# First rows of w_sp split ahead of the token mixer's last tile, and the w_out and first z loads queued behind the transposes of those rows

## The chip, the cores and the metric

The kernel runs on one core of a Trainium2 chip. The metric is the device time of one execution, in microseconds (us); a kernel's time is the median of its runs. The engines are PE (matmul; PEld is its weight load), DVE (vector), ACT (activation), POOL and SP; nearly all DMAs of this kernel are issued by SP, one after the other, in the order of SP's instructions.

## The reference

Two kinds of layer alternate over x of shape 2048 x 640: a segmented attention `_A_ref` and a gated MLP `_B_ref`, each behind a layernorm and added to x, and this twice. The change touches the MLP alone:

```python
def _B_ref(x, w_in, w_sp, b_sp, w_out):
    z = _gelu(jnp.einsum("bsd,df->bsf", x, w_in))
    z1 = z[..., :Fh]                                   # Fh = 864
    z2 = _layernorm(z[..., Fh:], axis=-1)
    g = jnp.einsum("ts,bsf->btf", w_sp, z2) + b_sp[None, :, None]
    return jnp.einsum("bsf,fd->bsd", z1 * g, w_out)

x = x + _A_ref(_layernorm(x), ...)
x = x + _B_ref(_layernorm(x), B_w_in, B_w_sp, B_b_sp, B_w_out)
x = x + _A_ref(_layernorm(x), ...)
x = x + _B_ref(_layernorm(x), B_w_in, B_w_sp, B_b_sp, B_w_out)
```

`w_sp` is 2048 x 2048 and mixes the tokens, so all of z2 has to be there before the first row of g is done.

## The kernel before

Every operand of a matmul is split into a high and a low f16 part, and a product is three matmuls (high by high, high by low, low by high). Each of the two layer pairs runs three phases, so that every phase runs twice; "first call" and "second call" below are the two calls of a phase.

`phase1a` is the attention. `phase1b` goes over 16 tiles of 128 tokens. For each it normalizes, turns the tile by a DMA transpose (`th`), and multiplies with the two halves of `w_in`: `w_in_half(1)` fills PSUM tile `zp1`, from which `z2_half` makes z2 (gelu on ACT, L301; layernorm on DVE with a power on POOL; the high part `zh` on ACT, L303; the low part `zl` on DVE, L304). `w_in_half(0)` fills `zp0`, from which `z1_half` makes z1 (gelu on ACT, L308) and stores it (L309, `z1_d[t]`). zh and zl of all 16 tiles stay in SBUF. The tile worked on last is number 11 (`ts`), called "the last tile" here. The profile leaves out buffer numbers, so it writes z for z1 and z2, zp for zp0 and zp1, cz for cz1, cx for cx1 and x for x1.

`phase2` goes over 16 tiles of 128 rows of w_sp.

- `rows(t)` loads 128 rows (`wr`, 1 MB, one buffer, L355), takes the largest magnitude of each row on DVE (`am`, L357), makes a power of two from it (`ivw`, L362), and splits the rows in two halves of 1024 columns: high part on ACT (`wn`, L367), low part on DVE (`wn`, L368), and one DMA transpose for each half (L369) that turns it into `wt` (two buffers).
- `spatial(t)` loads z1 of the tile (`cz1`, 432 KB, L375), multiplies `wt` with zh and zl (96 matmuls into `gp`, L380; k runs over the 16 token tiles, and the second half of wt is needed from k = 8), adds the bias on ACT (`u`, L383), multiplies with z1, splits the result like the rows (`un`, L393 and L394), and turns it by a DMA transpose (`ut`, L396).
- `tail(t)` loads x (`cx1`, 320 KB, L404), multiplies `ut` with w_out (42 matmuls into `cyp`, L409), adds x and stores.

In `phase2`, rows(0) is recorded first, under a high priority; then w_out is loaded (`g.wu.load`): in the first call as seven pieces `wst` through two buffers, which ACT and DVE split (L72, L73) and SP stores away for the second call (L111, L113); in the second call as the four stored parts (L96, L98; 960 + 120 KB for each of `wuh` and `wul`, 2.2 MB in all). Then spatial(t), rows(t+1) and tail(t-1) follow for each t. In the first call the next attention's first work (`nxt.early`) is recorded from t = 8 on.

A scheduler sets the order on each engine, from priorities, dependences and a timing model; each engine and SP then work strictly in that order. In phase1a and phase1b the order on PE is as written. Tiles of phase2 lie partly in the space of phase1b's tiles, and the first instruction that writes such a place waits until phase1b's last reader is done. With each of SP's DMAs stand the semaphores it waits for; of these, two matter here: in the first call the second cz1 load (L375) waits for the last matmul of zp0 of the last tile, and in the second call the first w_out load (L96) waits for that matmul.

## Time and profile before

| | us |
|---|---|
| three runs | 2442.37, 2444.76, 2446.39 |
| median | 2444.76 |
| profiled execution, its time | 2440.32 |
| profiled execution, its span | 2438.6 |
| PE busy in the span | 2218.2 (91%) |
| phase2, first call: first matmul of `gp` | 863.79 |
| phase2, second call: first matmul of `gp` | 2045.13 |

The profiled execution took 2440.32 us, 1.7 us more than its span and 4.4 us less than the median of the runs. A row of the timeline gives the start in us from the span's start, the duration, engine, line, operation, output<-input, how many instructions are merged, and in brackets how long the engine sat idle before it and what ended that. SP rows carry the engine name SPq, and their duration is the time SP was held by the issue, not that of the transfer. A row of the windows gives, for a stretch, each engine's busy time and number of instructions, then the granted PE clock as a share of full speed, the mean busy share of the DMA engines, and what they moved in GB/s.

### The profile page before, as it was taken

The numbers are of one execution on the slowest core, as the hardware profiler recorded it, in microseconds if no ns is written. First come the engines' busy times: TensorE is split into PE (matmuls) and PEld (weight loads), VectorE is DVE, ScalarE is ACT, GpSimd is POOL, SyncE is SP. The second block draws the span as 40 slices with busy tenths as digits, with TensorE's granted clock in tenths as the row PEclk, the third lists the DMA queues.
The fourth block names the chain that finished last, engine by engine and source line by source line (L and its number), as shares of the span: only waits on it lengthen the run. The fifth ranks groups of instructions, "written<-read, shape, count | busy, mean of one in ns | idle before, by whom it ended". The sixth has DMA issues, their size and how long they took to land.

```text
span 2438.6 us, 50718 instructions
## 1 busy us (share of the span) xinstructions
PE 2218.2 (91%) x20682; PEld 1319.0 (54%) x20682; DVE 1434.3 (59%) x2766; ACT 1133.7 (46%) x1388; POOL 936.1 (38%) x728
## 2 busy tenths in 40 slices
PE   3698789999899989999997989999988997999998
PEld 2355455666555545555554556565654554555554
DVE  8668878777654555444326777877764452454441
ACT  3278777777632222212124988777762221121110
POOL 3168678888610100000002988887871010000000
PEclk9899999999999999999999999999998998999999
DMA  6824634344553488766445253443455345665762
GB/s 196 214 57 109 162 115 122 93 117 133 146 143 107 113 223 206 171 157 164 114 127 133 77 119 88 113 109 93 123 160 124 88 108 165 163 169 155 175 127 58
DMA packets 502505, 325.00 MB, mean 133 GB/s; under 512 B 408512, under 2 KB 443456, under 8 KB 497152
## 3 DMA queue, kind: packets, MB, share of 16 engines
q1 hardware_dynamic: 502272, 321.76, 51.4%
q8 instruction: 162, 2.65, 0.5%
q14 instruction: 71, 0.58, 0.1%
HBM read 148.25 MB, written 85.34 MB: 96 GB/s over the span
## 4 chain that ended last, share of the span: by engine, by line
PE 60%; DVE 11%; DMA 11%; ACT 7%; issue 5%; POOL 3%; SPq 3%; ACTq 0%; DVEq 0%; POOLq 0%
PE gp L380 16%; PE zp L295 14%; PE cyp L409 6%; PE pv L909 3%; PE yps L666 3%; PE kps L690 3%; DMA wr<-in_B_w_sp_dram 3%; PE vps L633 3%; PE mp L856 3%; PE qps L690 3%; ACT PH L882 2%; ACT P L865 2%; PE es L856 2%; POOL PL L883 2%; DVE mx L872 2%
## 5 line engine op out<-in xcount | busy, mean ns | idle before, releaser
L883 POOL TENSOR_TENSOR PL<-P,PH 128x1280 f16<-128x1280 f32 x248 | 649.8, 2621 | 155.2 <-ACT PH L882 145.6
L380 PE MATMUL gp<-zh,wt 128*128 128x432 f16 x2048 | 466.5, 348 | 24.0 <-DMA wt<-wn 24.0
L872 DVE TENSOR_REDUCE mx<-mp 128x2 f32<-128x1024 f32 (+3 forms) x512 | 409.4, 818 | 108.1 <-PE mp L828 106.2
L380 PEld LDWEIGHTS <-wt 128*128 128x128 f16 x3072 | 301.8, 98 | 286.5 <-DMA wt<-wn 25.7
L865 ACT ACTIVATE P<-es,sc 128x1024 f32<-128x1024 f32 (+1 forms) x384 | 370.3, 964 | 128.5 <-PE es L828 122.6
L882 ACT CAST PH<-P 128x1280 f16<-128x1280 f32 x256 | 320.5, 1253 | 19.0 <-PE pv L909 12.0
L295 PEld LDWEIGHTS <-th 128*128 128x128 f16 x1920 | 188.9, 99 | 177.8 <-issue 11.7
L380 PE MATMUL gp<-zl,wt 128*128 128x432 f16 x1024 | 272.8, 348 | 0.0
L395 POOL MEMSET un<- 128x64 f16 x32 | 4.8, 151 | 675.7 <-DMA ut<-un 588.9
L205 POOL TENSOR_TENSOR lnrs<-lnve,mhalf 128x1 f32<-128x1 f32 x96 | 58.6, 618 | 484.6 <-DVE lnve L204 459.6
L856 PEld LDWEIGHTS <-qk 60*128 60x128 f16 (+1 forms) x2048 | 93.0, 94 | 222.2 <-issue 155.1
L357 DVE TENSOR_REDUCE am<-wr 128x1 f32<-128x2048 f32 x32 | 73.2, 2286 | 214.7 <-DMA wr<-in_B_w_sp_dram 214.6
L383 ACT ACTIVATE u<-gp,bsp,un 128x864 f32<-128x864 f32 x32 | 34.2, 1068 | 355.5 <-PE gp L380 355.5
L409 PE MATMUL cyp<-wuh,ut 128*128 128x320 f16 (+1 forms) x896 | 166.8, 303 | 15.4 <-DMA ut<-un 15.4
L633 PE MATMUL vps<-wvh,xt 128*128 128x320 f16 x640 | 156.3, 310 | 22.5 <-DMA xt<-xnhl 13.8
L856 PE MATMUL es<-qk 64*128 64x512 f16 (+3 forms) x1024 | 135.2, 299 | 41.6 <-ACT P L865 26.9
L409 PEld LDWEIGHTS <-ut 128*128 128x128 f16 (+1 forms) x1344 | 132.6, 99 | 73.7 <-DMA ut<-un 17.4
L909 PE MATMUL pv<-vs,PL 128*128 128x41 f16 x2560 | 163.8, 181 | 7.3 <-POOL PL L883 4.5
L909 PE MATMUL pv<-vs,PH 128*128 128x41 f16 x2560 | 167.8, 182 | 1.2 <-DVE ab L925 1.2
L828 PEld LDWEIGHTS <-big 64*128 64x128 f16 x3072 | 141.7, 95 | 49.8 <-issue 3.1
L856 PE MATMUL mp<-qk 60*128 60x512 f16 (+3 forms) x1024 | 137.8, 306 | 31.1 <-DVE mx L872 28.6
L367 ACT ACTIVATE wn<-wr,ivw 128x1024 f16<-128x1024 f32 x64 | 71.9, 1144 | 194.6 <-DVE ivw L362 111.1
(182 smaller groups left out, 4138.5 us busy)
## 6 DMA issues: line engine op xcount, KB each, us to landing
wr<-in_B_w_sp_dram SPq DMA_DIRECT2D x32, 1024.0 KB
qk<-st SPq DMA_DIRECT2D x256, 120.0 KB
x<-x SPq DMA_DIRECT2D x56, 320.0 KB
z<-z SPq DMA_DIRECT2D x32, 432.0 KB
cz<-z SPq DMA_DIRECT2D x32, 432.0 KB
xt<-in_A_x_dram SPq DMA_DIRECT2D x32, 320.0 KB
st<-qhl SPq DMA_DIRECT2D x40, 256.0 KB
st<-khl SPq DMA_DIRECT2D x40, 256.0 KB
```

The lines of the kernel that those rows point to most:

```text
L295: nc.tensor.matmul(zp[:, n, :FHH], a[:, k, :], b[:, k, c:c + FHH], start=(k == 0 and j == 0), stop=(k == KD - 1 and j == 2))
L380: nc.tensor.matmul(gp[:, n, :FHH], wt[:, k // 8, a, k % 8, :], b[:, k, n * FHH:(n + 1) * FHH], start=(k == 0 and j == 0), stop=(k == NT - ...
L409: nc.tensor.matmul(yp[:, n, :320], a[:kn[k], k, :], b[:kn[k], k, n * 320:(n + 1) * 320], start=(k == 0 and j == 0), stop=(k == KO - 1 and ...
L633: nc.tensor.matmul(ps, a[:, k, c], b[:, k, n * 320:(n + 1) * 320], start=(i == 0), stop=(i == 14))
L690: nc.tensor.matmul(ps, a[:, k, c], b[:, k, :], start=(i == 0), stop=(i == 14))
L828: nc.tensor.matmul(out, g.big[r, 64 - 64 * s:192 - 64 * s], mk, start=False, stop=s == 1, skip_group_check=True)
L856: nc.tensor.matmul(out[:, h, o:o + w], a[r, ac], b[r, bc], start=o == 0, stop=False, skip_group_check=True)
L865: nc.scalar.activation(P[:, :, 512 * c:512 * c + ew], es[:, :, :ew], AF.Exp, scale=g.esc)
L872: nc.vector.tensor_reduce(self.mx[m][:, :, i], mp[:, :, o:o + w], AX.X, ALU.max)
L882: nc.scalar.copy(PH, P[:, h])
L883: (nc.gpsimd if h == 0 or n < self.N - self.TAIL else nc.vector).tensor_tensor(PL, P[:, h], PH, ALU.subtract)
L909: nc.tensor.matmul(pv[:, i, h, :], x[:, c:c + 128], v[:, j, h0 + h, :], start=(j == 0 and x is PH), stop=(j == i and x is PL), skip_group_ ...
```

## The change

The split of the first rows (both halves, ACT and DVE) is placed ahead of two instructions of the last tile of phase1b: the gelu of z2 on ACT and the layernorm's last step on DVE get a dependence on the split, which is one of order alone (no semaphore). The w_out load and the first spatial, and with them the first z load, are recorded so that their DMAs are issued behind the second transpose of the first rows.

```diff
 def layernorm(g, xt, out, d, nch, mult=1.0):
     mv, rs = layernorm_stats(g, xt, d, nch, mult)
-    g.nc.vector.tensor_scalar(out, xt, mv[:, 0:1], rs, ALU.subtract, ALU.mult)
+    return g.nc.vector.tensor_scalar(out, xt, mv[:, 0:1], rs, ALU.subtract, ALU.mult)
...
-            nc.scalar.activation(z2.rearrange("p (n c) -> p n c", n=2), zp[:, :, :FHH], AF.Gelu_apprx_tanh, scale=g.zi[1])
-            layernorm(g, z2, z2, FH, 2, ZS)
+            i = nc.scalar.activation(z2.rearrange("p (n c) -> p n c", n=2), zp[:, :, :FHH], AF.Gelu_apprx_tanh, scale=g.zi[1])
+            j = layernorm(g, z2, z2, FH, 2, ZS)
+            g.last = i.ins, j.ins
...
-                nc.scalar.activation(hl[:, 0], wr[:, c], AF.Identity, scale=ivw)
-                nc.vector.scalar_tensor_tensor(hl[:, 1], wr[:, c], ivw, hl[:, 0], ALU.mult, ALU.subtract)
-                nc.sync.dma_start(wt[:, i].rearrange("p l k c -> p (l k) c"), hl.rearrange("p l c -> p (l c)"), transpose=True)
-            return wt, un
+                done = (nc.scalar.activation(hl[:, 0], wr[:, c], AF.Identity, scale=ivw),
+                        nc.vector.scalar_tensor_tensor(hl[:, 1], wr[:, c], ivw, hl[:, 0], ALU.mult, ALU.subtract))
+                for ins, behind in zip(done, g.last):
+                    if t == 0:
+                        tc.add_manual_dep(behind, ins.ins.name, mybir.DependencyInfo(
+                            mybir.DependencyClass.NoSync, mybir.DependencyReason.DATA), reason="first rows lead")
+                last = nc.sync.dma_start(wt[:, i].rearrange("p l k c -> p (l k) c"), hl.rearrange("p l c -> p (l c)"), transpose=True).ins
+            return wt, un, last
...
         with tc.high_priority(offset=HP):
             wt = rows(0)
-        for _ in g.wu.load(sp, D):
-            pass
+        with tc.issue_after(wt[2]):
+            for _ in g.wu.load(sp, D):
+                pass
         pend = None
         for t in range(NT):
-            u = spatial(t, wt)
+            with tc.issue_after(wt[2]) if t == 0 else ExitStack():
+                u = spatial(t, wt)
```

No instruction is added or taken away; the scheduler places them in another order. From L302 on, a line of the changed kernel stands up to 7 lines later than before.

On ACT, at the end of phase1b in the first call, before (L303 is zh, L308 the gelu of z1, L301 that of z2, L367 the split of rows, L72 that of w_out):

```order
L308 ACTIVATE z_12835<-zp_12804,sc 128x864
L301 ACTIVATE z_12869<-zp_12838,sc 128x864
L303 CAST zh<-z_12869 128x864
L367 ACTIVATE wn<-wr,ivw 128x1024 x2
L308 ACTIVATE z_12914<-zp_12883,sc 128x864
L72 ACTIVATE wuh<-wst,iv 128x640 x6
L367 ACTIVATE wn<-wr,ivw 128x1024 x2
```

and with the change:

```order
L309 ACTIVATE z_12835<-zp_12804,sc 128x864
L368 ACTIVATE wn<-wr,ivw 128x1024 x2
L301 ACTIVATE z_12869<-zp_12838,sc 128x864
L309 ACTIVATE z_12914<-zp_12883,sc 128x864
L304 CAST zh<-z_12869 128x864
L72 ACTIVATE wuh<-wst,iv 128x640 x4
L368 ACTIVATE wn<-wr,ivw 128x1024 x2
```

The split of the first rows moves from behind the last tile's zh to ahead of its z2 gelu; zh of that tile now comes behind the z1 gelu; and four pieces of w_out instead of six stand ahead of the split of the second rows. DVE's order moves alike, with one difference: there, the third piece of w_out stands between the row maximum and `ivw` of the second rows.

On SP at the same place, before, each DMA with the semaphores it waits for (the number in a name is a buffer's; a DMAHW semaphore is that of an earlier DMA):

```order
L309 DMA z_0_10<-z_12835 128x864 [waits Activation_49]
L106 DMA wst<-in_B_w_out_dram 128x640 [waits DMAHW6_49,PE_49]
L106 DMA wst<-in_B_w_out_dram 128x640 [waits DMAHW7_49]
L375 DMA cz_13026<-z_0_0 128x864 [waits DMAHW2_49]
L375 DMA cz_13167<-z_0_1 128x864 [waits DMAHW4_49,DMAHW1_49,PE_49]
L404 DMA cx_13308<-x_0_0 128x640
L404 DMA cx_13497<-x_0_1 128x640 [waits DMAHW3_49]
L369 DMA_TRANSPOSE wt<-wn 128x16x128 [waits DVE_49]
L369 DMA_TRANSPOSE wt<-wn 128x16x128 [waits DMAHW5_49,DVE_49]
L309 DMA z_0_11<-z_12914 128x864 [waits DMAHW6_49,Activation_49]
```

and with the change:

```order
L310 DMA z_0_10<-z_12835 128x864 [waits Activation_49]
L409 DMA cx_13308<-x_0_0 128x640 [waits DMAHW6_49,DMAHW4_49,PE_49]
L409 DMA cx_13497<-x_0_1 128x640 [waits DMAHW7_49,DMAHW2_49]
L374 DMA_TRANSPOSE wt<-wn 128x16x128 [waits DVE_49]
L374 DMA_TRANSPOSE wt<-wn 128x16x128 [waits DMAHW1_49,DVE_49]
L310 DMA z_0_11<-z_12914 128x864 [waits Activation_49]
L106 DMA wst<-in_B_w_out_dram 128x640 [waits DMAHW3_49]
L106 DMA wst<-in_B_w_out_dram 128x640
L380 DMA cz_13026<-z_0_0 128x864 [waits DMAHW5_49]
L356 DMA wr<-in_B_w_sp_dram 128x2048 [waits DMAHW6_49]
L380 DMA cz_13167<-z_0_1 128x864 [waits DMAHW7_49]
```

The two x loads of the tails are in neither group that the change holds back, and now come first. The first of them takes over the wait on PE that the second cz load had: for the last matmul of zp0 of the last tile. The transposes of the first rows stand right behind it.

On SP in the second call, with the change:

```order
L310 DMA z_1_10<-z_28382 128x864 [waits Activation_49]
L409 DMA cx_28818<-x_1_0 128x640 [waits DMAHW6_49,DMAHW2_49,DMAHW0_49]
L409 DMA cx_29007<-x_1_1 128x640 [waits DMAHW3_49,PE_49]
L374 DMA_TRANSPOSE wt<-wn 128x16x128 [waits DVE_49]
L374 DMA_TRANSPOSE wt<-wn 128x16x128 [waits DMAHW5_49,DVE_49]
L310 DMA z_1_11<-z_28461 128x864 [waits Activation_49]
L96 DMA wuh<-w_uh 128x3840 [waits DMAHW7_49]
L98 DMA wuh<-w_uh 96x640
L96 DMA wul<-w_ul 128x3840 [waits DMAHW1_49]
L98 DMA wul<-w_ul 96x640 [waits DMAHW2_49]
L380 DMA cz_28536<-z_1_0 128x864 [waits DMAHW3_49]
L356 DMA wr<-in_B_w_sp_dram 128x2048 [waits DMAHW4_49]
```

Before, the four w_out loads and two cz loads stood ahead of the first transpose there, and the load of the second rows (L355) came right behind the store of z_1_11; now w_out and a cz load stand between that store and the second rows. Further on in the second call, the transpose of the first `ut` comes ahead of those of the third rows instead of behind them, and on PE the first `cyp` group comes right behind the second `gp` group instead of 11 matmuls into the third. In the first call, the transpose of the fourth `ut` comes ahead of a load of rows instead of behind it. From the eighth rows on, SP's order in phase2 is the same as before in both calls.

More of the change, by code (lines that the diff above doesn't have):

```diff
@@ L366, in rows @@
                 hl = ph.tile([128, 2, 1024], F16, tag="wn", name="wn")
-                nc.scalar.activation(hl[:, 0], wr[:, c], AF.Identity, scale=ivw)
-                nc.vector.scalar_tensor_tensor(hl[:, 1], wr[:, c], ivw, hl[:, 0], ALU.mult, ALU.subtract)
-                nc.sync.dma_start(wt[:, i].rearrange("p l k c -> p (l k) c"), hl.rearrange("p l c -> p (l c)"), transpose=True)
-            return wt, un
+                done = (nc.scalar.activation(hl[:, 0], wr[:, c], AF.Identity, scale=ivw),
[6 more added lines that the diff above has]
+            return wt, un, last
         def spatial(t, wt):
-            wt, un = wt
+            wt, un, _ = wt
             z1 = p2.tile([128, FH], F32, tag="z1", name="cz1")
```

## The prediction

> **What bounds the kernel now.** I read the page first, its busy shares and its chain of waits, and then its costliest groups.
>
> ```profile
> PE 2218.2 (91%) x20682; PEld 1319.0 (54%) x20682; DVE 1434.3 (59%) x2766; ACT 1133.7 (46%) x1388; POOL 936.1 (38%) x728
> ...
> PE 60%; DVE 11%; DMA 11%; ACT 7%; issue 5%; POOL 3%; SPq 3%; ACTq 0%; DVEq 0%; POOLq 0%
> ...
> L380 PE MATMUL gp<-zh,wt 128*128 128x432 f16 x2048 | 466.5, 348 | 24.0 <-DMA wt<-wn 24.0
> ...
> L409 PE MATMUL cyp<-wuh,ut 128*128 128x320 f16 (+1 forms) x896 | 166.8, 303 | 15.4 <-DMA ut<-un 15.4
> ```
>
> PE is busy 91% of the span, and in phase2 it waits for one thing only: DMA transposes, 24.0 us for `wt` and 15.4 us for `ut`, 39.4 us in all. What this change moves can win no more than that, and the slow starts that follow some of these waits. Next I read PE's timeline through both calls of phase2 and kept the rows with an idle time of over half a microsecond in brackets, and some without for the length of a group.
>
> ```profile
> 863.79 0.90 PE L380 MATMUL gp<-zh,wt 128*128 128x432 f16 x2 [7.37 <-DMA wt<-wn]
> 887.30 0.54 PE L380 MATMUL gp<-zh,wt 128*128 128x432 f16 x2 [3.78 <-DMA wt<-wn]
> 906.51 0.43 PE L409 MATMUL cyp<-wuh,ut 128*128 128x320 f16 x2
> 912.22 0.53 PE L380 MATMUL gp<-zh,wt 128*128 128x432 f16 x2
> 929.74 0.43 PE L409 MATMUL cyp<-wuh,ut 128*128 128x320 f16 x2
> 935.45 0.53 PE L380 MATMUL gp<-zh,wt 128*128 128x432 f16 x2
> 980.06 0.45 PE L409 MATMUL cyp<-wuh,ut 128*128 128x320 f16 x2 [3.70 <-DMA ut<-un]
> 1004.98 0.43 PE L409 MATMUL cyp<-wuh,ut 128*128 128x320 f16 x2
> ...
> 2045.13 0.90 PE L380 MATMUL gp<-zh,wt 128*128 128x432 f16 x2 [12.23 <-DMA wt<-wn]
> 2065.32 0.54 PE L380 MATMUL gp<-zh,wt 128*128 128x432 f16 x2 [0.61 <-DMA wt<-wn]
> 2087.39 0.45 PE L409 MATMUL cyp<-wuh,ut 128*128 128x320 f16 x2 [2.38 <-DMA ut<-un]
> 2133.66 0.45 PE L409 MATMUL cyp<-wuh,ut 128*128 128x320 f16 x2 [1.64 <-DMA ut<-un]
> 2159.88 0.31 PE L409 MATMUL cyp<-wuh,ut 128*128 128x320 f16 x1 [2.82 <-DMA ut<-un]
> ```
>
> An undisturbed `gp` group takes 929.74 - 912.22 = 17.52 us, a `cyp` group 935.45 - 929.74 = 5.71, a tile 23.23. The first group of the first call ran from 863.79 to 887.30 - 3.78 = 883.52, which is 19.73: 2.21 too long. The second took 906.51 - 887.30 = 19.21: 1.69 too long. From 980.06 to 1004.98 it is 24.92, again 1.69 over a tile. The first group of the second call took 2065.32 - 0.61 - 2045.13 = 19.58: 2.06 over. So a stall of 3.7 us or more costs about 2 us behind it as well; after 2.38 us there is nothing of the kind: 2133.66 - 2087.39 = 46.27 is two tiles less the 11 matmuls that already ran (46.46 - 2.01), plus the stall of 1.64, but for 0.2. It is the granted clock, 0.50 in the gap by the windows (row below).
>
> **The change part by part.** First call. The rows' split, in the timelines of ACT and DVE:
>
> ```profile
> 850.98 0.98 ACT L301 ACTIVATE z<-zp,sc 128x864 f32<-128x864 f32 x1 [4.50 <-PE zp L295]
> 855.91 2.18 ACT L367 ACTIVATE wn<-wr,ivw 128x1024 f16<-128x1024 f32 x2
> ...
> 851.99 1.12 DVE L202 BATCH_NORM_STATS2 lnst<-z 128x6 f32<-128x432 f32 x2 [5.85 <-ACT z L301]
> 857.08 2.48 DVE L368 SCALAR_TENSOR_TENSOR wn<-wr,ivw,wn 128x1024 f16<-128x1024 f32 x2
> ```
>
> Moved ahead of the last z2, the split's 2.18 us fit ACT's 4.50 idle, and its 2.48 us DVE's 5.85. I cost the move at nothing; without that cover it would delay the last tile's zh and zl, which PE reads only at k = 15, 16 us into the first group. The split is then done before 851 instead of at 857.08 + 2.48 = 859.6. The transposes, however, are SP's, here its timeline and the second rows' maximum on DVE:
>
> ```profile
> 851.46 5.31 SPq L375 DMA_DIRECT2D cz<-z  x2
> 856.81 0.91 SPq L404 DMA_DIRECT2D cx<-x  x2
> 858.40 5.63 SPq L369 DMA_TRANSPOSE wt<-wn  x2
> 866.43 0.52 SPq L355 DMA_DIRECT2D wr<-in_B_w_sp_dram  x1
> 880.94 4.25 SPq L369 DMA_TRANSPOSE wt<-wn  x1
> ...
> 873.98 2.29 DVE L357 TENSOR_REDUCE am<-wr 128x1 f32<-128x2048 f32 x1 [2.15 <-DMA wr<-in_B_w_sp_dram]
> ```
>
> The second cz load holds SP until 856.8, just after zp0's last matmul (863.79 - 7.37 = 856.42). The first cx load now has that wait, and both transposes are queued behind it. So they go out at about 856.4 + 2 x 0.45 = 857.3 instead of 858.40: all the early split buys is 1.1 us. From issue to use it was 863.79 - 858.40 = 5.39; the first group would start near 862.7 and end at 882.4. **Gain of the first group: 1.1** (0 to 1.5; the upper end if the two cz loads' traffic no longer slows it).
>
> The second group waits for the second rows. Their load now follows transposes to about 862.9, the z store, two w_out pieces and a cz load: issued near 865.4 rather than 866.43, but behind 0.44 + 0.66 + 0.44 MB instead of 0.44 + 0.66, so I let it land as now, 873.8. Then DVE's order bites: the third w_out piece stands ahead of `ivw`, and its load may go out only when the first piece is split (near 871.4), behind the rows and a cz load. At the rate of the windows (below) it lands near 875.5; ACT and DVE split it by 877.3, the rows' split starts at 877.5, the transpose goes out at 880 against 880.94. It took 887.30 - 880.94 = 6.36 to land, behind two stores of w_out parts (0.98 MB each); these now come later, so I take 5.14 (2065.32 - 2060.18, an undisturbed one below): start at 885.2, 2.1 earlier. The stall before it is 885.2 - 882.4 = 2.8, between 2.38 (clock kept) and 3.70 (clock lost), so I take half of the 1.69: 0.8 more. **Gain up to the second group's end: 2.9, of which 1.1 is the first group's** (-2 to 5: third w_out piece 5 us late, or none late).
>
> The fourth `cyp` stalled 3.70 and lost 1.69 of clock, 5.39, for a reason that its SP rows show:
>
> ```profile
> 971.06 0.38 SPq L355 DMA_DIRECT2D wr<-in_B_w_sp_dram  x1
> 971.54 2.68 SPq L396 DMA_TRANSPOSE ut<-un  x1
> ```
>
> Its transpose stood right behind a 1 MB load. It now stands ahead of it. Against that, the third rows' load goes out only behind the first `ut` transpose and the w_out stores, near 892.7, some 4 us later than now; following the chain on (load 7, maximum and split 5, pair of transposes 5), I find the third `wt` and the third and fourth `ut` each landing within about 1 us of when PE wants them. I take 3 us for these three. **Gain 2.4** (-3 to 5.4). First call: 2.9 + 2.4 = 5.3.
>
> Second call. SP's timeline shows what is ahead of the first transposes; DVE's row is the second rows' landing, and two windows show the DMA engines (the last three figures are clock, DMA share and GB/s):
>
> ```profile
> 2032.93 0.32 SPq L96 DMA_DIRECT2D wuh<-w_uh  x1
> ...
> 2035.69 9.45 SPq L369 DMA_TRANSPOSE wt<-wn  x2
> ...
> 2046.14 0.44 SPq L355 DMA_DIRECT2D wr<-in_B_w_sp_dram  x1
> ...
> 2060.18 5.09 SPq L369 DMA_TRANSPOSE wt<-wn  x2
> ...
> 2054.55 2.29 DVE L357 TENSOR_REDUCE am<-wr 128x1 f32<-128x2048 f32 x1 [18.50 <-DMA wr<-in_B_w_sp_dram]
> ...
> 2036.00:2038.00 2.00, 0.00 (x0) 0.00 (x0) 0.05 (x1) 0.00 (x0) 0.00 (x0) 0.50 1.05 403
> 2056.00:2058.00 2.00, 2.00 (x13) 1.07 (x12) 1.50 (x6) 0.32 (x1) 0.00 (x0) 1.00 0.00 0
> ```
>
> w_out (2.2 MB) and two cz loads, 3.1 MB, go out from 2032.93 and keep the transposes waiting for 9.45 us. With the change only one cx load is ahead: issue at 2033.4, landing 5.14 later at 2038.6 instead of 2045.13. The first group starts 6.5 us earlier. But the 3.1 MB are not gone: the z store, w_out and a cz load now stand ahead of the second rows' load. The pair lands by about 2042 (an estimate: 5.14 for the first half, some 3 more for the second), then 0.44 + 2.2 + 0.44 + 1.05 = 4.1 MB at 400 GB/s is 10.3 us, and with the rest of the path a landing near 2053.9, against 2054.55. The DMA engines were idle at 2056, so this is when they are done with the same work in another order. The second group then starts at 2054 + 10.77 (2065.32 - 2054.55) = 2064.7, only 0.6 earlier, while the first now ends at 2038.6 + 19.6 = 2058.2. The 12-us gap is cut in two of 5.7 and 6.5, and the second one loses clock that the 0.61 did not: -2.0. **Second group's end: 1.4 later** (4.8 later if the bytes move at 300 GB/s, to 0.6 earlier).
>
> A rule of the Trainium skill bears on these slow starts ("TensorE: Matmul & The Clock Gate", Part 1): PE falls to half clock after an idle window of about 3.4 us and needs about as long a busy one to rise. By it a slow start costs at most 1.7 us (an estimate, half of 3.4), where this trace has 1.69 to 2.21, and the 2.8-us stall of the first call would cost none, as 2.38 did here; the sum below would be 1.1 us better, 2433.7.
>
> The first `cyp` of the second call waited 2.38 for `ut`, and two later ones 1.64 and 2.82. SP's rows:
>
> ```profile
> 2083.36 1.54 SPq L396 DMA_TRANSPOSE ut<-un  x1
> 2085.00 1.03 SPq L355 DMA_DIRECT2D wr<-in_B_w_sp_dram  x1
> ...
> 2123.14 0.49 SPq L355 DMA_DIRECT2D wr<-in_B_w_sp_dram  x1
> ...
> 2124.28 6.84 SPq L396 DMA_TRANSPOSE ut<-un  x1
> ```
>
> The first `ut` went out at 2083.36, behind the third rows' pair. It now stands ahead of that pair, near 2066 (an estimate: some 8 us of ACT and DVE behind the first group's end), while PE asks for it at 2084: **gain 2.4** (0 to 2.4). The fourth rows' load, at 2085.00 behind that `ut`, then no longer waits for it and goes out near 2082; with the steps as long as they are, the fifth tile's chain comes 4 to 5 us ahead of before, PE's work 1 us. The third `ut` held SP for 6.84 us behind the load of 2123.14. Its stall of 1.64 and the next one's 2.82 would go but for some 0.8: **gain 3.7** (0 to 4.5). Second call: -1.4 + 2.4 + 3.7 = 4.7.
>
> **Sum.** 5.3 + 4.7 = 10.0 us. The profiled execution would take 2440.32 - 10.0 = 2430.3; the runs' median is 4.4 above it, so 2444.76 - 10.0 = 2434.8, predicted as 2435. Later phases only shift: the attention that follows starts from phase2's last tiles, and no stall of phase2 lies between 980 and its end in the first call. POOL's order changes only among its memsets of `un`.
>
> **The rivals.** *The wait only moves.* The first groups start earlier, the second ones as before, and the `ut` stalls stay, because they belong to a DMA queue that has the same bytes to move. For it: 856.42 as SP's release, and DMA idle at 2056 whatever the order. Against it: three of those stalls have a changed order. Price: 2.9 in the first call, -1.4 + 2.4 in the second, minus about 1 of new stalls: gain 3, 2441.8.
>
> *The second rows become the bound.* w_out stands ahead of them in both calls. In the first the third piece lands as late after its issue as the rows did (873.98 - 866.43 = 7.55, so at 879 instead of 875.5), which puts the transpose at 883.5 and the group at 889, 1.7 later than now; 0.4 of clock and 1 of new stalls come on top. In the second the 4.1 MB move at 300 GB/s, 4.8 lost, 2.4 won back at `ut`. Stalls at 980, 2133 and 2159 as before. Sum 3.1 + 2.4 = 5.5 slower, 2450. It decides once the second `wt` lands after about 888 and 2066. For it: DVE's and SP's new order, and the bytes that now stand ahead of the load. Against: the 403 GB/s that the row shows.
>
> *More.* All waits for `ut` go and the second group of the first call comes 5 earlier: 18 us, 2427.
>
> **How the numbers follow.** Forecast 0.55, the wait only moves 0.24, second rows bound 0.14, more 0.07. A change of this kernel under 0.2%, 4.9 us, can't be told from none. Within the forecast about 0.06 falls short of it, and of the first rival 0.04 passes it: faster 0.60, same 0.26, slower 0.14. Range: 2427, all terms at their upper ends, to 2447, between the two rivals; the forecast's own is 2430 to 2440.
>
> **What would show it.** In the profile of the changed kernel: the first-rows split on ACT right behind the z1 gelu near 846, and the transpose all the same at 857; first groups near 862.7 and, by the gap before them, 5.7 us behind phase1b's last matmul in the second call; half clock after that in the second group there; its `wt` landing 26 us after the first; no idle time at the fourth `cyp` of the first call. Wrong it would be if the transposes left before zp0's last matmul, if the second rows landed more than 3 us off, or if `ut` stalls of more than 3 us in a call remain.

## The result and the profile after

| | us |
|---|---|
| the change, median of 14 runs | 2445.00 |
| before, median of 14 runs beside it | 2444.53 |
| ratio, with its 95% interval | 0.9999 (0.9988 to 1.0011) |
| profiled execution of the change, its time and its span | 2445.33, 2443.6 |

The change makes no difference that can be measured. A second set of runs (e10 below) gave 0.9988 (0.9974 to 1.0002). The forecast was 10 us less than before. The median lies within the range on record, 2427 to 2447, but the gain that was forecast did not come: as the table further down shows, the second call gained what was expected, the first lost nearly as much, and the two cancel.

The page of the changed kernel, the lines that stand against the first ones of the prediction:

```profile
PE 2224.8 (91%) x20682; PEld 1323.1 (54%) x20682; DVE 1437.5 (59%) x2766; ACT 1134.6 (46%) x1388; POOL 936.9 (38%) x728
...
L385 PE MATMUL gp<-zh,wt 128*128 128x432 f16 x2048 | 468.0, 349 | 22.5 <-DMA wt<-wn 22.5
...
L414 PE MATMUL cyp<-wuh,ut 128*128 128x320 f16 (+1 forms) x896 | 168.1, 305 | 12.6 <-DMA ut<-un 12.6
```

PE's idle time at `wt` and `ut` fell from 39.4 to 35.1 us, so 4.3 us of waiting are gone. But PE was busy 6.6 us longer (2224.8 against 2218.2) with the same 20682 matmuls. Half of that, 3.3 us, falls in the two stretches of phase2 that the table below compares (156.9 to 158.9 us and 130.5 to 131.9); the other half falls ahead of phase2 and between its calls, in work that the change does not touch. Where the waits and the slow matmuls of phase2 are shows in PE's timeline through its two calls. Here and below, only the rows with a wait or the start of a group are shown:

```profile
868.78 0.90 PE L385 MATMUL gp<-zh,wt 128*128 128x432 f16 x2 [6.46 <-DMA wt<-wn]
890.64 0.54 PE L385 MATMUL gp<-zh,wt 128*128 128x432 f16 x2 [2.09 <-DMA wt<-wn]
908.17 0.43 PE L414 MATMUL cyp<-wuh,ut 128*128 128x320 f16 x2
916.30 0.54 PE L385 MATMUL gp<-zh,wt 128*128 128x432 f16 x2 [2.26 <-DMA wt<-wn]
935.51 0.43 PE L414 MATMUL cyp<-wuh,ut 128*128 128x320 f16 x2
985.02 0.45 PE L414 MATMUL cyp<-wuh,ut 128*128 128x320 f16 x2 [2.89 <-DMA ut<-un]
992.41 0.53 PE L385 MATMUL gp<-zh,wt 128*128 128x432 f16 x2
1013.16 0.71 PE L414 MATMUL cyp<-wuh,ut 128*128 128x320 f16 x2 [3.06 <-DMA ut<-un]
1020.45 0.53 PE L385 MATMUL gp<-zh,wt 128*128 128x432 f16 x2
1037.97 0.43 PE L414 MATMUL cyp<-wuh,ut 128*128 128x320 f16 x2
...
2047.91 0.90 PE L385 MATMUL gp<-zh,wt 128*128 128x432 f16 x2 [5.29 <-DMA wt<-wn]
2073.32 0.90 PE L385 MATMUL gp<-zh,wt 128*128 128x432 f16 x2 [6.40 <-DMA wt<-wn]
2093.11 0.43 PE L414 MATMUL cyp<-wuh,ut 128*128 128x320 f16 x2
2164.76 0.45 PE L414 MATMUL cyp<-wuh,ut 128*128 128x320 f16 x2 [1.80 <-DMA ut<-un]
```

The start of the first `gp` group less its idle time is the end of phase1b's last matmul: 868.78 - 6.46 = 862.32, and 2042.62 in the second call. Before it was 856.42 and 2032.90. Nothing that the change does lies ahead of 862.32 on PE; across the twelve profiles of this study that end lies anywhere from 854.75 to 862.32, and both of these have the early split (e4 and the change). So two profiles are compared by stretches that begin at one event. Counted from phase1b's end:

| start of | before | change | gained so far |
|---|---|---|---|
| first call: first `gp` group | 7.37 | 6.46 | 0.9 |
| second `gp` group | 30.88 | 28.32 | 2.6 |
| first `cyp` group | 50.09 | 45.85 | 4.2 |
| second `cyp` group | 73.32 | 73.19 | 0.1 |
| sixth `cyp` group | 171.78 | 175.65 | -3.9 |
| second call: first `gp` group | 12.23 | 5.29 | 6.9 |
| second `gp` group | 32.42 | 30.70 | 1.7 |
| fifth `cyp` group | 150.22 | 145.38 | 4.8 |

Behind the sixth `cyp` of the first call and the fifth of the second, the two profiles run in step. The second call gained 4.8 us, as forecast (4.7). The first call gained 4.2 up to its first `cyp` and then lost 8.1. In the sum 1 us is left, less than the runs can tell. A second profile of the change (e10) gives 174.8 and 145.4 for the last rows of the two calls, so these numbers repeat within about 1 us.

### The profile page after: what moved, and what is told of

It is laid out like the page before. It is cut to its first block, busy times and chain, and to the rows that moved or that the text cites. A ratio compares the mean times of both kernels' runs of the same rounds, so it can differ in the third digit from the quotient of the medians.

```text
span 2443.6 us, 50712 instructions
## 1 busy us (share of the span) xinstructions
PE 2224.8 (91%) x20682; PEld 1323.1 (54%) x20682; DVE 1437.5 (59%) x2766; ACT 1134.6 (46%) x1388; POOL 936.9 (38%) x728
## 4 chain that ended last, share of the span: by engine, by line
PE 62%; DVE 11%; DMA 10%; ACT 7%; issue 5%; POOL 3%; SPq 2%; ACTq 0%; DVEq 0%; POOLq 0%
PE gp L385 16%; PE zp L295 14%; PE cyp L414 6%; PE pv L916 3%; PE yps L673 3%; PE kps L697 3%; PE vps L640 3%; PE mp L863 3%; PE qps L697 3%; DMA wr<-in_B_w_sp_dram 2%; ACT PH L889 2%; PE es L863 2%; ACT P L872 2%; DVE mx L879 2%; DMA ut<-un 2%
```

## The experiments

Two numbers are given for each kernel: the starts of the sixth `cyp` group in the first call and of the fifth in the second, from phase1b's end. The ratios are to runs of the kernel before that were taken beside each set; their medians were 2444.53 us for the change, 2444.55 for e1 to e4, 2440.59 for e5 to e8 and 2442.78 for e9 and e10, so medians of different sets can't be compared directly.

| | first call | second call | median, us | ratio to before (95%) |
|---|---|---|---|---|
| before | 171.8 | 150.2 | | |
| the change | 175.7 | 145.4 | 2445.00 | 0.9999 (0.9988 to 1.0011) |
| e1, the split alone | 174.6 | 152.3 | 2446.08 (one run) | |
| e2, the hold-back alone | 177.5 | 148.5 | 2443.06 (one run) | |
| e3, second call only | 172.4 | 146.1 | 2440.12 | 0.9983 (0.9970 to 0.9996) |
| e4, third rows early | 175.4 | 147.0 | 2442.13 | 0.9992 (0.9977 to 1.0007) |
| e5, `ut` ahead of the rows' load | 166.7 | 144.3 | 2431.47 | 0.9961 (0.9946 to 0.9977) |
| e6, the same without the change | 166.9 | 144.0 | 2434.62 | 0.9965 (0.9951 to 0.9979) |
| e7, x loads held back too | 162.0 | 138.6 | 2423.29 | 0.9928 (0.9911 to 0.9944) |
| e8, all of it | 157.5 | 132.2 | 2408.55 | 0.9866 (0.9850 to 0.9882) |
| e9, e7 without the early split | 169.7 | 145.6 | 2434.52 | 0.9967 (0.9954 to 0.9981) |
| e10, the change again | 174.8 | 145.4 | 2439.78 | 0.9988 (0.9974 to 1.0002) |

### Which part does what: e1, e2, e3

e1 takes the hold-back out:

```diff
-        with tc.issue_after(wt[2]):
+        with ExitStack():
             for _ in g.wu.load(sp, D):
                 pass
...
-            with tc.issue_after(wt[2]) if t == 0 else ExitStack():
+            with ExitStack():
                 u = spatial(t, wt)
```

> Only the split of the first rows is moved ahead of the last tile; w_out and the z loads are not held back, so SP's order is that of before. Measured are, in the profile, the times from the last matmul of phase1b to the sixth cyp group of phase2's first call (before 171.8 us, change 175.7) and to the fifth cyp group of the second call (before 150.2, change 145.4). Theory (SP's order sets everything, the split is under cover): 171.8 and 150.2, each within 0.5, because the first transposes still stand behind w_out and the z loads. Rival 1 (the early split itself delays the last tile's z2 and with it zh and zl, which costs the first call what it lost): the first call 174 or more, with a stall of PE inside the first gp group at k = 15. Rival 2 (what was seen is one execution's chance): both numbers off by several us, in any direction.

Measured: 174.6 and 152.3. The theory's numbers were missed by 2.8 and 2.1, and rival 1 has the right number in the first call, but not by its mechanism: there is no stall inside the first group. PE's timeline of e1 shows what happened:

```profile
862.74 0.90 PE L385 MATMUL gp<-zh,wt 128*128 128x432 f16 x2 [7.44 <-DMA wt<-wn]
885.78 0.54 PE L385 MATMUL gp<-zh,wt 128*128 128x432 f16 x2 [3.36 <-DMA wt<-wn]
903.31 0.43 PE L414 MATMUL cyp<-wuh,ut 128*128 128x320 f16 x2
952.21 0.72 PE L414 MATMUL cyp<-wuh,ut 128*128 128x320 f16 x2 [2.28 <-DMA ut<-un]
959.55 0.53 PE L385 MATMUL gp<-zh,wt 128*128 128x432 f16 x2
```

and POOL's timeline of the kernel before dates the landing of the same `ut` there:

```profile
951.59 0.15 POOL L395 MEMSET un<- 128x64 f16 x1 [26.71 <-DMA ut<-un]
```

The first group starts as late as before (7.44 against 7.37): with the z loads ahead of the transposes, the early split buys nothing there. The second group's stall of 3.36 cost no clock (903.31 - 885.78 = 17.53, an undisturbed group), so the first `cyp` came 2.1 earlier than before. The third `cyp` then stalled for 2.28 and lost another 1.63 of clock (959.55 - 952.21 = 7.34 against 5.71). The end of PE's wait dates the landing of its transpose, 952.21. Where PE does not wait, POOL does: its memset of `un` can start only when the transpose that reads `un` is done, so a memset whose wait ended with that transpose dates the landing. Before, that was 951.59. Counted from phase1b's end, this `ut` landed at 95.2 before and at 96.9 in e1, and PE asked for it at 96.6 before and at 94.6 in e1. So it was late all along and covered by 1.4 us. Of the stall of 2.28, 0.5 was uncovered by the gain ahead of it; the other 1.7 is a later landing, because the transpose went out 1.8 later (88.4 against 86.6). Why it did is not shown. In the second call, 1.69 of the 2.1 is clock: PE waited 2.41 us at its first `cyp` and lost 1.69 behind it, where before it waited 2.38 and lost nothing.

e2 takes the early split out and keeps the hold-back:

```diff
                 for ins, behind in zip(done, g.last):
-                    if t == 0:
+                    if False:
```

> Only the hold-back: SP's order is that of the change, the split of the first rows stands where it stood before, behind the last tile's zh. Theory: the first call loses as the change did, 175.7 plus up to 2 (the split ends some 2 us later than SP is free for it); the second call 145.4 plus up to 3, for the same reason. So the hold-back explains the loss of the first call and nearly all of the gain of the second. Rival 1 (the early split makes the loss): the first call 172 or less. Rival 2 (the early split makes the gain of the second call): the second call near 150.

Measured: 177.5 and 148.5, at the upper end of what the theory allowed. The hold-back alone makes the loss of the first call, but only 1.7 of the 4.8 us that the second gains. With the early split on top, the change is 1.9 and 3.1 us better than e2 in the two calls.

e3 gives the first call the order of before:

```diff
+        second = g.wu.made
...
-        with tc.issue_after(wt[2]):
+        with tc.issue_after(wt[2]) if second else ExitStack():
...
-            with tc.issue_after(wt[2]) if t == 0 else ExitStack():
+            with tc.issue_after(wt[2]) if second and t == 0 else ExitStack():
...
-                    if t == 0:
+                    if t == 0 and g.wu.made:
```

> The change in the second call alone; the first call has the order of before on every engine. Theory (the two calls have opposite signs): first call 171.8 within 0.5, second call 145.4 within 0.5, and the median 4 to 5 us below the kernel before, a ratio of 0.998. Rival 1 (the second call's gain is given back behind the fifth cyp group, or in the rest of the program): ratio 1.000. Rival 2 (chance): the second call's number near 150.

Measured: 172.4 and 146.1, ratio 0.9983. Both numbers are 0.6 to 0.7 over the theory's, a little outside its half microsecond, and the ratio is as forecast. With the change in the second call alone, the kernel gains; that the first call loses rests on the stretches of the profiles (the change, e2 and e10), as the intervals of e3 and of the change overlap.

### What the first call loses: e4

SP's timeline in the first call of the change: the second and third rows' loads, and then three `ut` transposes with the load of rows that stands next to each.

```profile
862.35 0.79 SPq L409 DMA_DIRECT2D cx<-x  x2
863.20 5.54 SPq L374 DMA_TRANSPOSE wt<-wn  x2
...
871.81 0.43 SPq L356 DMA_DIRECT2D wr<-in_B_w_sp_dram  x1
...
885.72 3.14 SPq L374 DMA_TRANSPOSE wt<-wn  x1
...
900.45 1.00 SPq L356 DMA_DIRECT2D wr<-in_B_w_sp_dram  x1
...
952.62 1.57 SPq L401 DMA_TRANSPOSE ut<-un  x1
...
972.37 0.46 SPq L356 DMA_DIRECT2D wr<-in_B_w_sp_dram  x1
...
974.71 6.25 SPq L401 DMA_TRANSPOSE ut<-un  x1
...
1004.54 0.33 SPq L356 DMA_DIRECT2D wr<-in_B_w_sp_dram  x1
1005.60 1.31 SPq L401 DMA_TRANSPOSE ut<-un  x1
```

The landings of these three, by POOL's timeline:

```profile
956.71 0.15 POOL L400 MEMSET un<- 128x64 f16 x1 [2.08 <-DMA ut<-un]
985.11 0.15 POOL L400 MEMSET un<- 128x64 f16 x1 [28.25 <-DMA ut<-un]
1013.16 0.15 POOL L400 MEMSET un<- 128x64 f16 x1 [1.28 <-DMA ut<-un]
```

Two explanations offer themselves. One: the third rows' load left at 900.45, 38.1 us behind phase1b's end, where before it was 888.81 - 856.42 = 32.4, and all that follows is late. The other: a transpose lands late whenever a 1 MB load stands just ahead of it. The third `ut`, with the last such load 19.8 us ahead, took 956.71 - 952.62 = 4.1 us to land; the fourth, 2.3 us behind a load, took 10.4; the fifth, 1.1 us behind one, 7.6. e4 tells them apart. It puts the third rows' load ahead of the four stores of w_out (`g.wu.stores`) and of the first `ut` (`g.ut0`), and says nothing of the later loads and `ut`s:

```diff
-            nc.sync.dma_start(wr, w_sp[t * 128:(t + 1) * 128, :])
+            i = nc.sync.dma_start(wr, w_sp[t * 128:(t + 1) * 128, :]).ins
+            if t == 2 and g.wu.stores:
+                for behind in g.wu.stores + [g.ut0]:
+                    tc.add_manual_dep(behind, i.name, mybir.DependencyInfo(
+                        mybir.DependencyClass.NoSync, mybir.DependencyReason.DATA), reason="third rows lead")
+                g.wu.stores = []
```

> The change, and in the first call the load of the third rows stands ahead of the four stores of w_out and of the first ut transpose instead of behind them; the rest of SP's order to the tenth DMA behind is the same. Theory (the third rows' load, 5.7 us late, makes the stalls at the third gp group, 2.26, and at the fourth and fifth cyp, 2.89 and 3.06, and the slow clock behind them): the load goes out some 30 us behind phase1b's end instead of 38, these three stalls go but for 1 to 2 us in all, and the sixth cyp group starts at 168 to 170 instead of 175.7; the median 8 to 11 us below the kernel before (ratio 0.9955 to 0.997). Rival 1 (the stores of w_out and the ut transposes are what the queue is short of, and the wait only moves to the first ut): a new stall at the first or second cyp group and 174 to 176. Rival 2 (the stalls at the fourth and fifth cyp come from their own loads, not from the chain of the third): the stall of 2.26 goes, the others stay, 173.

Measured: 175.4, nothing gained. The load went out 30.0 us behind phase1b's end, as wanted, and the third `wt` no longer stalled. But these are SP's rows further on,

```profile
941.49 0.39 SPq L357 DMA_DIRECT2D wr<-in_B_w_sp_dram  x1
...
942.54 7.11 SPq L407 DMA_TRANSPOSE ut<-un  x1
```

PE's,

```profile
952.43 0.72 PE L422 MATMUL cyp<-wuh,ut 128*128 128x320 f16 x2 [5.41 <-DMA ut<-un]
982.04 0.45 PE L422 MATMUL cyp<-wuh,ut 128*128 128x320 f16 x2 [3.26 <-DMA ut<-un]
```

and POOL's:

```profile
952.52 0.15 POOL L406 MEMSET un<- 128x64 f16 x1 [26.65 <-DMA ut<-un]
```

Now the third `ut` stands 1.1 us behind a load, takes 952.52 - 942.54 = 10.0 us to land, and PE waits for it 5.41 us. The scheduler's order explains it: in e4 the loads of rows and the `ut` transposes stand on SP in the order of the kernel before, with the sixth rows' load just ahead of the third `ut`, the eighth just ahead of the fourth, and the fifth `ut` ahead of the ninth rows' load. So the third `ut` collides, the fourth still does (0.5 us behind a load, a stall of 3.26), and the fifth no longer does and has no stall. The theory of the late third rows falls but for the one stall at the third `wt`. Rival 2, that each stall belongs to the load next to it, is right about the cause; its number (173) took the loads to stay where they were, and missed that one collision went and a new one came.

### The collisions: e5 and e6

e5 keeps the change and queues the load of rows t+3 behind the transpose of `ut` t:

```diff
+        uts = []
+
+        def behind_ut(i, t):
+            if t >= 3:
+                tc.add_manual_dep(i, uts[t - 3].name, mybir.DependencyInfo(
+                    mybir.DependencyClass.NoSync, mybir.DependencyReason.DATA), reason="ut leads")
...
-            nc.sync.dma_start(wr, w_sp[t * 128:(t + 1) * 128, :])
+            behind_ut(nc.sync.dma_start(wr, w_sp[t * 128:(t + 1) * 128, :]).ins, t)
...
-            nc.sync.dma_start(ut.rearrange("p l k c -> p (l k) c"), hl.rearrange("p l c -> p (l c)"), transpose=True)
+            uts.append(nc.sync.dma_start(ut.rearrange("p l k c -> p (l k) c"), hl.rearrange("p l c -> p (l c)"), transpose=True).ins)
```

> The change, and in both calls the load of rows t+3 is issued behind the transpose of ut t. Theory (a ut transpose that is issued within 3 us behind a 1 MB load of rows lands 7.6 to 10.4 us after its issue, one with no load ahead of it 4.1; these collisions, not the third rows' load, cost the first call its gain): the stalls at the fourth and fifth cyp of the first call (2.89 and 3.06, with some 4 of slow clock) and the 1.80 in the second go, the third wt's 2.26 stays. Sixth cyp group of the first call 166 to 168 us behind phase1b's end (before 171.8, change 175.7), fifth of the second call 143.6 (before 150.2, change 145.4); ratio to before 0.995 to 0.997. Rival 1 (the rows' chain is the bound, and a later load makes wt late in the place of ut): new stalls at gp groups in the first eight tiles, 174 or more. Rival 2 (what is gained in the first tiles is lost behind them): the numbers as by the theory, but ratio 0.998 or more.

Measured: 166.7 and 144.3, ratio 0.9961, as the theory had it. The stalls of 3.06 and 1.80 are gone and that of 2.89 is down to 1.98, with no clock lost behind it. What is left of it is the same thing with smaller transfers: this `ut` landed 7.6 us behind its issue (973.27 to 980.85), right behind a store of x, a z load and two x loads, 1.4 MB in four pieces. Of the 9.0 us that the first call gained on the change, 1.8 are luck: the third `wt` stalled much as in the change (2.18), but with no slow clock behind it, for which the edit gives no reason.

e6 does the same edit to the kernel before.

> The kernel before, without the change, and with the load of rows t+3 issued behind the transpose of ut t. By the theory of the collisions, the stalls of 3.70 in the first call and of 1.64 and 2.82 in the second go: sixth cyp group 166.4 us behind phase1b's end (before 171.8), fifth of the second call 145.8 (before 150.2), ratio 0.996. Rival 1 (the rows' chain is the bound): new stalls at gp groups, 171 or more. Rival 2 (the collision is chance, and another transpose takes its place): some ut still lands over 7 us behind its issue.

Measured: 166.9 and 144.0, ratio 0.9965. PE's rows at the fourth `cyp` of the first call and at the first, third and fourth of the second, where before it waited 3.70, 2.38, 1.64 and 2.82:

```profile
977.39 0.44 PE L416 MATMUL cyp<-wuh,ut 128*128 128x320 f16 x2
...
2084.11 0.45 PE L416 MATMUL cyp<-wuh,ut 128*128 128x320 f16 x2 [0.60 <-DMA ut<-un]
2128.57 0.43 PE L416 MATMUL cyp<-wuh,ut 128*128 128x320 f16 x2
2151.80 0.43 PE L416 MATMUL cyp<-wuh,ut 128*128 128x320 f16 x2
```

In both calls no `ut` that can be dated lands over 6.7 us behind its issue, so rival 2 did not come. The order of the rows' loads and the `ut` transposes, with nothing else touched in the source, wins 0.35%, about 8.5 us, where the whole change was forecast to win 10. The collisions were there before the change; in the first call the change moved the tiles so that two of them met PE in the place of one.

### What holds the first transposes back: e7, e9

e7 is the change with the x loads of the first three tails queued behind the first transposes too:

```diff
             if pend is not None:
-                tail(*pend)
+                with tc.issue_after(first) if t < 3 else ExitStack():
+                    tail(*pend)
```

where `first` is the second transpose of the first rows.

> The change, and the first two x loads of the tails are queued behind the first transposes as well; then no DMA ahead of the transposes waits for zp0's last matmul. Theory (that wait, which the first x load inherits, is all that keeps the first transposes back): they go out some 8 us ahead of phase1b's end, and the first gp group starts within 1.5 us of it in both calls (change 6.5 and 5.3). The second rows' load still stands behind w_out and sets the second group: its start about 20 us (first call) and 22 us (second call) behind phase1b's end, against 28.3 and 30.7 with the change; ratio 0.990 to 0.994. Rival 1 (the wait moves to the second group in full): its start 28 and 30 as with the change, ratio 0.999 or more. Rival 2 (the transposes ahead of phase1b's end collide with its own z stores or th transposes and make zp wait): phase1b longer, a stall of PE at zp.

Measured: ratio 0.9928. SP's timeline in its first call,

```profile
851.12 4.35 SPq L374 DMA_TRANSPOSE wt<-wn  x2
```

and PE's in both calls:

```profile
858.51 0.53 PE L385 MATMUL gp<-zh,wt 128*128 128x432 f16 x2
879.68 0.58 PE L385 MATMUL gp<-zh,wt 128*128 128x432 f16 x2 [3.49 <-DMA wt<-wn]
...
2022.38 0.53 PE L385 MATMUL gp<-zh,wt 128*128 128x432 f16 x2
2047.25 0.90 PE L385 MATMUL gp<-zh,wt 128*128 128x432 f16 x2 [7.19 <-DMA wt<-wn]
```

The transposes leave 7.4 us ahead of phase1b's end in both calls, and PE goes from `zp` to `gp` without a gap. The second rows then set the second group, at 21.2 and 24.9 us (20 and 22 were expected). Phase1b has no new stall.

e9 is e7 without the early split:

```diff
-                    if t == 0:
+                    if False:
```

> The kernel of e7 without the early split: the first transposes are free of the wait on zp0, but the split of the first rows stands behind the last tile's zh as before. Theory (the early split is worth nothing by itself, e1, and is what lets the transposes leave ahead of phase1b's end once that wait is gone): the split's first half ends some 2 us behind phase1b's end, the first group starts 6 to 7.5 us behind it in both calls (e7 under 1.5), the second at 27 to 30 (e7 21.2 and 24.9), and the time is that of the change or a little less, a ratio of 0.996 to 1.000 to before (e7 0.9928). Rival (the x loads alone make the gain of e7, by what they took of SP and the queues): first group under 3 us and ratio 0.994 or less.

Measured: first groups at 6.4 in both calls (the change 6.5 and 5.3), second groups at 27.7 and 32.3, the latter beyond the 30 that was expected, and ratio 0.9967, just inside what the theory allowed. The freed x loads without the early split don't bring the first group of the first call forward, and neither does the early split without them (the change, e1); together they do, and e7 is 0.4% below e9. The split is what makes the transposes ready, and the wait on `zp0` is what kept them back all the same.

### Everything together: e8

e8 is e7 with e5's edit, and with the second rows' load (`fetch(1)`, the load taken out of `rows`) ahead of the last z store (`g.zst`) and of w_out; the first z load and the x loads of the first tails are queued behind it too. Its own part of the edit:

```diff
         with tc.issue_after(wt[2]):
+            wr1, lead = fetch(1)
+        tc.add_manual_dep(g.zst, lead.name, mybir.DependencyInfo(
+            mybir.DependencyClass.NoSync, mybir.DependencyReason.DATA), reason="second rows lead")
+        with tc.issue_after(lead):
             for _ in g.wu.load(sp, D):
                 pass
```

> The change, the x loads behind the first transposes, the second rows' load ahead of the last z store and of w_out, and the load of rows t+3 behind the transpose of ut t. Theory (three causes, each with its own share: the wait on zp0 ahead of the transposes, w_out ahead of the second rows, the collisions of ut with the rows' loads): no wait for wt in either call beyond 1.5 us at the first group, no wait for ut over 0.5; sixth cyp group of the first call 153 us behind phase1b's end (change 175.7), fifth of the second call 130 (change 145.4); 37 us in all against the change, ratio 0.983 to 0.987. Rival 1 (w_out, now behind the second rows, becomes the bound of the first cyp group): a stall of 5 us or more there, ratio 0.987 to 0.991. Rival 2 (the time is given back behind phase2): numbers as by the theory, ratio 0.992 or more.

Measured: 157.5 and 132.2, median 2408.55, ratio 0.9866 (0.9850 to 0.9882), 1.3% less than before, where the change alone won nothing. The page's group of `gp` has 2.9 us of waiting for `wt` left, all at the second group of the second call, where none over 1.5 was expected:

```profile
L398 PE MATMUL gp<-zh,wt 128*128 128x432 f16 x2048 | 462.5, 346 | 2.9 <-DMA wt<-wn 2.9
...
L427 PE MATMUL cyp<-wuh,ut 128*128 128x320 f16 (+1 forms) x896 | 167.0, 304 | 11.4 <-DMA ut<-un 11.2
```

The two numbers are 4.5 and 2.2 later than expected, because some `ut`s still land 5 to 6 us behind their issue and PE, now ahead, waits for them (1.25, 1.62 and 2.47 in the first call); no stall over 0.5 was expected.

### The change once more: e10

> The change once more, for a second profile of it. Theory: the first call's sixth cyp group starts 174 to 177 us behind phase1b's end and the second call's fifth 144 to 147, as the order of SP sets them; a ut transpose that is issued within 3 us behind a rows' load lands over 7 us later. Phase1b's own end, which the change does not touch, differs by some us from 862.3 and 2042.6. Rival (the first profile was chance): the first call near 167, as the prediction had it.

Measured: 174.8 and 145.4. The same stalls are at the same groups: 2.11 and 2.25 at the second and third `gp`, 2.09 and 2.79 at the fourth and fifth `cyp`. The loss of the first call was not chance. Phase1b's end was at 860.55 and 2043.16.

## Why the prediction went as it did

**The first transposes (right).** They were to leave right behind `zp0`'s last matmul in spite of the early split. The split was done at 855.9 on DVE, and the transposes went out at 863.20, 0.9 us behind phase1b's end. The gain was 0.9 where 1.1 was forecast, and e7 shows the wait that was named as the cause. One detail was wrong without effect: the last tile is number 11, so its zh is read at k = 11 and not at k = 15.

**The second group of the first call (right, a little small).** The transpose was to leave 23.6 us behind phase1b's end and left at 23.4; the group was to start at 28.8 and started at 28.3. Its stall of 2.09 cost no clock, where half of 1.69 was put down. So the gain at its end was 4.2 instead of 2.9.

**The `ut`s and the third `wt` of the first call (wrong).** This is the step that failed: "Its transpose stood right behind a 1 MB load. It now stands ahead of it", and "I take 3 us for these three". The first sentence is true of the load of the eighth rows, and stops there. SP's rows of the kernel before, around its fourth and fifth `ut`:

```profile
955.79 0.33 SPq L355 DMA_DIRECT2D wr<-in_B_w_sp_dram  x1
...
988.22 1.53 SPq L396 DMA_TRANSPOSE ut<-un  x1
...
991.42 0.49 SPq L355 DMA_DIRECT2D wr<-in_B_w_sp_dram  x1
```

The load of the seventh rows, which left at 955.79 and so 15.8 us ahead of the fourth `ut` (971.54), has slipped to 2.3 us ahead of it (972.37 and 974.71). And the fifth `ut`, which before left at 988.22, ahead of the ninth rows' load at 991.42, now stands right behind that load (1004.54 and 1005.60). That swap was in SP's order before anything ran; the account of the change ahead of the prediction leaves it out (it has the order as unchanged from the eighth rows on), and the prediction does not name the fifth `ut` at all. The third rows' load left at 38.1 us behind phase1b's end, where 36.3 was reckoned. Of the three near-misses that were put at 3 us together, the third `ut` came in time, and the third `wt` and the fourth `ut` became full stalls; the fifth `ut` was another. Each had a slow start behind it:

- third `wt`: 2.26, and 935.51 - 916.30 - 17.52 = 1.69 of clock
- fourth `ut`: 2.89, and 1.68 up to the next group (992.41 - 985.02 = 7.39 against 5.71)
- fifth `ut`: 3.06, and 1.58

Together 13.2 us (2.26 + 1.69 + 2.89 + 1.68 + 3.06 + 1.58) in the place of the 5.39 of before; idle times under 0.2 us make up the rest of the 8.1. The term was put at a gain of 2.4 and measured a loss of 8.1, outside its own range, which ended at -3. The prediction expected no idle time at the fourth `cyp` of the first call, and said that it would be wrong if `ut` stalls of more than 3 us in a call remained; 5.95 remained.

**The second call (right in its mechanism, and partly by luck in its sum).** Transposes 0.4 us behind phase1b's end (0.5 forecast), gap 5.29 (5.7), second rows landed at 2063.28 - 2042.62 = 20.7 (21.0), gap at the second group 6.40 (6.5) and 2.27 of clock behind it (2.0), first `ut` on time, and one stall of 1.80 left of two (0.8). Sum 4.8 against 4.7, but with two misses of about 1 us that cancel: the second group's end came about half a microsecond later where 1.4 was forecast (the first group, for one, lost 1.49 of clock and not the 2.06 of before), and the two later `ut` stalls gave 2.7 where 3.7 was forecast. At the third `ut` the load still stands 1.2 us ahead of the transpose, as before; the stall went because PE came for it 2.1 us after it had landed (2139.57 against 2137.51 at the latest). The bytes of w_out did not hold the second rows up beyond that, so the rival of the second rows did not come.

**The rival that came nearest** in the number is that the wait only moves (a gain of 3), but not as it was described. It put the first call at a gain of 2.9 less new stalls and the second at 1.0; they measured -3.9 and 4.8. Its reason was a queue with the same bytes to move. e5 and e6 move the same bytes and lose most of these waits: it is the order in which a transpose and a larger load reach the queue.

**The clock.** The prediction weighed 1.69 to 2.21 us of slow start behind a stall of 3.7 or more and none behind 2.38. By the Trainium skill ("TensorE: Matmul & The Clock Gate", Part 1) an idle window of about 3.4 us is needed. Here 2.25 (e10) and 2.26 (the change) at a `gp` group lost 1.70 and 1.69, and 3.36 (e1) lost none, so the measurements decide against a sharp bound at 3.4; see the last section. The prediction's estimate from that rule, at most 1.7 us for a slow start, does not hold either: behind a stall of 3.68 in e9, a `cyp` group took 8.50 instead of 5.71, 2.8 more.

## What to carry to other kernels

A DMA that is on the critical path is dated by what stands just ahead of it in the queue, so after any shift of the stages the pairs of a large load and a small transpose have to be found again, all of them, in the order of the list and in time; where a buffer leaves room, pin the order (transpose first) rather than let it fall out. When work is moved earlier, look for the first instruction in its queue that still waits for the old event: here an unrelated load took over that wait, and the gain stayed away until it was moved too. And before a stall is written off as gone, ask what was covered by it: time won ahead of a late transfer can uncover that transfer, as 0.5 us of it did in e1.

## What the runs showed of the hardware

**A `ut` transpose lands by what is ahead of it.** It took 4.1 us when only a pair of `wt` transposes had been issued in the 6.6 us ahead of it (952.62 to 956.71 in the change), 6.6 to 10.4 when a 1 MB load was issued up to 3 us ahead of it (ten cases that POOL's wait dates in three profiles: before, the change and e4), and 7.6 once behind four transfers of 0.3 to 0.4 MB (e5). The expectation of e5 had 7.6 as the least for the second kind, which is true of the first call alone: the 6.6 is the fourth `ut` of the second call before. Whether the transposes wait in the queue or move more slowly beside the load is not shown.

**The clock falls after shorter stalls than expected, and not every time.** These are the waits of PE for `wt` and `ut` in phase2 of the twelve profiles. Stalls up to 1.98 us cost no clock. From 2.09 to 3.41 us some cost 1.4 to 1.7 us and others nothing, at nearly the same length: 2.11 and 2.25 in the same call of e10 lost 0 and 1.70. From 3.49 us on all of them lost. The windows show it; each row is a stretch, the busy times of the engines, the granted clock and the DMA engines' share and rate. First the change behind its stall of 2.89:

```profile
985.02:987.00 1.98, 1.98 (x10) 1.24 (x11) 1.20 (x2) 1.78 (x3) 0.66 (x2) 0.66 0.01 4
987.00:989.00 2.00, 2.00 (x10) 1.09 (x8) 2.00 (x2) 1.15 (x2) 1.61 (x1) 0.50 0.00 0
```

and e9 behind one of 3.41:

```profile
976.30:978.30 2.00, 2.00 (x15) 1.46 (x16) 1.94 (x2) 1.07 (x2) 0.15 (x1) 1.00 0.72 247
```

Behind 2.89 the clock was 0.66 and 0.50 for 4 us, behind 3.41 it was full. What decides between them is open; it was not tried.
